# Reordering the first batch item of a Sinkhorn-sorted attention fused with a maxout feed-forward

## The chip, the cores and the metric

The kernel runs on one core of one Trainium2 chip. The metric is the device time of one execution, in microseconds. The time before is the median of 7 runs.

## What is computed

```
P = sort_net                              # 4 x 8 x 8 x 8, one 8x8 matrix for each item and head
for _ in range(5): P = exp(P - max); rows normalised; columns normalised
k_sorted, v_sorted = P applied over the 8 blocks of 96 tokens of k and v
scores = q_block . k_sorted_block^T / 8   # block by block, 96 x 96
x_attn = softmax(scores) . v_sorted       # 4 items x 768 tokens x (8 heads x 64)
h1 = x @ w1 ; h2 = x @ w2                 # 3072 tokens, 512 -> 1024
out = maximum(h1, h2) @ w_out             # 1024 -> 512
```

The kernel uses maximum(h1, h2) = relu(h1 - h2) + h2. It forms w1 - w2 once (`w_difference`, a quarter of the columns at a time), so that the first product needs one pass, and w2 @ w_out once (`w2_transposes`, `w_product`), so that h2 never appears.

## The kernel before

The four items (b) are processed one after the other, software-pipelined: while the feed-forward of item b runs, the attention of item b+1 is spread among its products. Item 0 has nothing to hide behind, so its order is written out by hand, statement by statement, at lines 682 to 713. All instructions of an engine run in the order in which they are written; `manual_schedule` keeps the written order, and the waits between engines are added by the framework.

The steps of one item, by the names used in the code and in the prediction:

- `sort_k(b, t)`, t = 0 to 2, and `sort_v(b, t)`, t = 0 to 3: block-diagonal products that mix the blocks of k and v, and an eviction on ACT or DVE into `kT` or `v_sb`. All value sorts must be evicted before the first values step.
- `q_transposes(b, half)`: for items 0 and 1 24 PE transposes (one more matmul ahead of them for item 0) and an eviction into `qT`; each half serves two of the four head pairs.
- `scores(b, u)` (SC, u = 0 to 7): 8 small matmuls and one exp on ACT. u = 4 * ih + hp, where hp is the head pair and ih the half of the blocks. hp 0 and 1 need the first half of q, hp 2 and 3 the second.
- `values(b, u)` (VA): 8 small matmuls, then a reciprocal and a multiplication on DVE, which give `x`.
- `x_transposes(b, t)` (TR): for item 0 8 PE transposes and an eviction into `xT`; for later items a DMA transpose on the SP queue. TR t needs values 2t and 2t+1. TR 0 and 1 serve token half 0, TR 2 and 3 token half 1.
- `moe_h(b, ch, t)`: the first product of token half ch, column tile t: 8 matmuls of 384 columns and a relu into `g`. `moe_h_products` issues a part of them: the parts (0, 2) need TR 0 only, the parts (1, 3) need TR 1. Tile t needs `w_difference(t)`. Differences 0 and 1 are on GpSimd (POOL), 2 and 3 on DVE.
- `w2_transposes(t, eng)`: 16 PE transposes and an eviction into `w2T`.

Every step that uses TensorE takes one of four PSUM tiles ("ps", two banks each); a step waits until the tile that it was given has been evicted. A number as the last argument of `scores`, `values` or `moe_h_products` puts that many columns of matmuls with zeros (`keep_streaming`) ahead of the step.

After the hand-written order come the selection copies and then the loop over items. In it `units` are the products of the feed-forward, and the planner adds `steps` of the next item in proportion to the units' costs. For item 0 units 0 and 1 are empty, units 2 to 7 are the remaining h tiles, units 8 to 11 the w products. `tail` names steps that follow a certain unit of item 0: the remaining work of item 0, the turning of v (`turn`), the block diagonals of the other items, the key sorts of item 1, and loads (`load_rest` is q of item 1 and k of item 2). Where an eviction has no engine given, `pick` chooses ACT or DVE from two running totals of planned time. All loads are issued by POOL, outputs by SP.

## Time and profile before

| what | value |
|---|---|
| median of 7 runs | 171.18 us (170.94 to 171.74) |
| profiled execution, its own time | 170.94 us |
| its span | 169.1 us |
| PE busy | 161.7 us (96% of the span) |
| ACT busy | 85.8 us (51%) |
| DVE busy | 75.8 us (45%) |
| POOL busy | 29.1 us (17%) |
| granted TensorE clock | 1.00 |
| DMA moved | 23.11 MB |

The profile is one execution, recorded by hardware. Times in its rows are in microseconds from the start of the span. PE is TensorE's matmuls and PEld its weight loads, DVE is VectorE, ACT is ScalarE, POOL is GpSimd, SP is SyncE. The rows of the timeline have start, length, engine, line, operation, output and inputs, shapes and count; in square brackets stands the engine's idle time before the row and what ended it. The ends of matmuls are modelled, so that neighbours seem to overlap; the distance from start to start says what a block costs.

### The profile page before, as it was taken

How to read it: one execution, taken by the hardware profiler on the slowest of the kernel's cores; microseconds unless marked ns; L12 is line 12 of the kernel's file. 1: busy time of each engine (PE TensorE's matmuls, PEld its weight loads, DVE VectorE, ACT ScalarE, POOL GpSimd, SP SyncE). 2: the span in 40 equal slices, each digit the busy share in tenths (PEclk: the TensorE clock that was granted, in tenths of full speed). 3: DMA queues.
4: the chain of work that ended last, by engine and by line, in shares of the span. 5: the costliest groups of instructions: out<-in, count | busy, mean ns of one | idle time of the engine just before them, and what ended most of it. 6: DMA issues, size and time to landing. Idle time of an engine off the chain costs nothing.

```text
span 169.1 us, 4528 instructions
## 1 busy us (share of the span) xinstructions
PE 161.7 (96%) x2001; PEld 97.2 (57%) x2019; DVE 75.8 (45%) x174; ACT 85.8 (51%) x104; POOL 29.1 (17%) x44
## 2 busy tenths in 40 slices
PE   7999989999999999999999999999999999999991
PEld 7948655567565554566664545557545455654451
DVE  5978765938363369437743443205442160000011
ACT  4587668686565352266775415456615416652020
POOL 7866584242312002100000000000000000000000
PEclk9999999999999999999999999999999999999999
DMA  3999999999999994899700253690054255000333
GB/s 51 204 203 198 200 207 207 218 204 206 217 214 205 205 206 94 174 156 237 159 0 4 63 155 131 95 292 17 0 35 139 47 176 171 0 0 0 124 141 111
DMA packets 30243, 23.11 MB, mean 137 GB/s; under 512 B 16720, under 2 KB 25168, under 8 KB 30224
## 3 DMA queue, kind: packets, MB, share of 16 engines
q0 software_dynamic: 10880, 12.59, 44.4%
q1 hardware_dynamic: 19200, 10.17, 24.7%
q8 instruction: 16, 0.26, 0.6%
q10 hardware_dynamic: 144, 0.07, 0.1%
q14 instruction: 3, 0.02, 0.0%
HBM read 25.17 MB, written 6.29 MB: 186 GB/s over the span
## 4 chain that ended last, share of the span: by engine, by line
PE 84%; DVE 9%; ACT 2%; issue 2%; DMA 1%
PE out_ps L617 35%; PE h_ps L590 23%; PE wc_ps L570 4%; PE o_ps L488 4%; PE k_ps L394 4%; PE s_ps L461 4%; PE v_ps L415 2%; PE fill_ps L82 2%; PE tq_ps L369 1%; ACT e L469 1%; PE v_ps L436 1%; DVE x L505 1%; PE tw_ps L551 1%; DVE qT L110 1%; DMA p_sb<-in_sort_net_dram 1%
## 5 line engine op out<-in xcount | busy, mean ns | idle before, releaser
L617 PE MATMUL out_ps<-wo_sb,g 128*128 128x512 bf16 (+2 forms) x188 | 47.0, 370 | 1.1 <-issue 0.3
L590 PE MATMUL h_ps<-xT,w_sb 128*128 128x384 bf16 x256 | 45.0, 326 | 0.4 <-ACT xT L108 0.3
L590 PEld LDWEIGHTS <-w_sb 128*128 128x128 bf16 x256 | 23.9, 98 | 16.1 <-issue 0.7
L108 ACT COPY o<-out_ps 128x1024 f32<-128x1024 f32 x11 | 11.1, 1012 | 40.4 <-issue 22.8
L604 ACT ACTIVATE g<-h_ps 128x768 bf16<-128x768 f32 x27 | 21.9, 811 | 15.0 <-PE h_ps L590 15.0
L469 ACT ACTIVATE e<-s_ps 96x768 bf16<-96x768 f32 x32 | 24.3, 804 | 7.7 <-PE s_ps L461 7.6
L617 PEld LDWEIGHTS <-g 128*128 128x128 bf16 x200 | 16.9, 98 | 15.7 <-DVE x L505 0.4
L617 PE MATMUL out_ps<-wc,xT 128*128 128x512 bf16 (+2 forms) x100 | 24.8, 370 | 0.1
L505 DVE TENSOR_TENSOR x<-o_ps,rs 96x512 bf16<-96x512 f32 x32 | 22.0, 687 | 1.1
L499 DVE RECIPROCAL rs<-o_ps 96x8 f32<-96x8 f32 x32 | 6.5, 202 | 32.2 <-PE o_ps L488 32.1
L617 PEld LDWEIGHTS <-xT 128*128 128x128 bf16 x100 | 9.6, 97 | 11.2
L488 PEld LDWEIGHTS <-e 96*128 96x128 bf16 x256 | 11.7, 98 | 7.0 <-ACT e L469 1.2
L488 PE MATMUL o_ps<-v_sb,e 96*128 96x65 bf16 x256 | 13.1, 193 | 0.4 <-ACT e L469 0.3
L652 DVE COPY o<-out_ps 128x512 f32<-128x512 f32 (+1 forms) x2 | 1.2, 624 | 25.0 <-PE out_ps L617 25.0
L110 DVE CAST v_sb<-v_ps 96x1024 bf16<-96x1024 f32 x8 | 9.6, 1215 | 4.2 <-PE v_ps L415 3.4
L110 DVE CAST kT<-k_ps 128x1024 bf16<-128x1024 f32 x5 | 6.0, 1222 | 11.3 <-PE k_ps L394 11.3
L461 PEld LDWEIGHTS <-kT 64*128 64x128 bf16 x256 | 6.3, 94 | 6.6 <-issue 5.9
L136 POOL DMA_DIRECT2D q_raw<-in_q_dram x7 | 6.4, 934 | 19.5 <-DVE rs L499 14.0
L108 ACT CAST v_sb<-v_ps 96x1024 bf16<-96x1024 f32 x8 | 8.0, 1006 | 3.2 <-PE v_ps L415 1.9
L461 PE MATMUL s_ps<-qT,kT 64*128 64x96 bf16 x256 | 9.0, 204 | 0.5 <-DVE qT L110 0.4
L82 PEld LDWEIGHTS <-fill 128*128 128x128 bf16 x99 | 8.2, 117 | 1.8 <-DVE fill L73 1.2
L82 PE MATMUL fill_ps<-fill 128*128 128x138 bf16 x88 | 7.5, 265 | 1.2 <-DVE fill L73 1.2
(77 smaller groups left out, 137.9 us busy)
## 6 DMA issues: line engine op xcount, KB each, us to landing
out_dram<-o SPq DMA_DIRECT2D x11, 512.0 KB, 3.0
k_raw<-in_k_dram POOLq DMA_DIRECT2D x12, 256.0 KB, 12.0
v_raw<-in_v_dram POOLq DMA_DIRECT2D x6, 384.0 KB, 11.7
q_raw<-in_q_dram POOLq DMA_DIRECT2D x3, 768.0 KB, 11.0
w_sb<-in_moe_w_dram POOLq DMA_DIRECT2D x4, 256.0 KB, 9.3
w_sb<-in_moe_w_dram POOLq DMA_DIRECT2D x2, 512.0 KB, 11.3
wo_sb<-in_moe_w_out_dram POOLq DMA_DIRECT2D x2, 512.0 KB, 14.8
v_raw<-in_v_dram POOLq DMA_DIRECT2D x3, 256.0 KB, 4.8
```

What stands on the lines that cost most here:

```text
L82: nc.tensor.matmul(ps[:, 0:w], w0, fill[:, 0:w], start=True, stop=True)
L108: nc.scalar.copy(out=out_ap, in_=in_ap)
L110: nc.vector.tensor_copy(out=out_ap, in_=in_ap)
L394: nc.tensor.matmul(ps[r0 : r0 + 64, m * 64 : (m + 1) * 64], kv[r0 : r0 + 64, t * 16 + m, :], bd_k[b][r0 : r0 + 64, :], start=True, stop=True,)
L461: nc.tensor.matmul(ps[:, h2 * 512 + ii * 128 : h2 * 512 + ii * 128 + BLK], kT[b][rows, (hp * 8 + i) * BLK : (hp * 8 + i) * BLK + 128], rhs ...
L469: nc.scalar.activation(out=e[:, 0 : 8 * BLK].rearrange("p (t c r) -> p t c r", t=8, r=R), in_=ps[0:BLK] .rearrange("p (t f) -> p t f", t=8 ...
L488: nc.tensor.matmul(ps[:, h2 * 512 + ii * 65 : h2 * 512 + (ii + 1) * 65], e[:, (h2 * 4 + ii) * BLK : (h2 * 4 + ii) * BLK + 128], v_sb[:, m0 ...
L505: nc.vector.tensor_tensor(out=x, in0=ov[:, :, :, 0:D], in1=rs.to_broadcast([BLK, 2, 4, D]), op=ALU.mult,)
L570: nc.tensor.matmul(ps[:, 0:512], w2T[:, fb, dmt * 128 : (dmt + 1) * 128], wo_sb[:, fb, :], start=(fb == 0), stop=(fb == NFB - 1),)
L590: nc.tensor.matmul(h_ps[t][:, m * 512 : m * 512 + TCH], w1_sb[:, hp, fb * 128 : (fb + 1) * 128], xT[:, b % 2, ch, hp % 2, hp // 2, :], sta ...
L604: nc.scalar.activation(out=g, in_=src, func=AF.Relu)
L617: nc.tensor.matmul(dst, g_tiles[b, ch, m // 2][:, m % 2, off : off + 128] if m < NFB else xT[:, b % 2, ch, hp % 2, hp // 2, off : off + 12 ...
```

## The change

In item 0, value sort 3 moves ahead of scores 0, scores 0 and 1 follow each other, and scores 4 moves ahead of values 0. The scores, values and x transposes of token half 1 move up among the h tiles: scores 5, 6 and 7 each one or more blocks earlier, values 6 and 7 and TR 2 into the hand-written order ahead of unit 2. The first half of h tile 1 is no longer issued apart: `moe_h(0, 0, 1)` is whole. The two w differences on DVE and the first w2 transposes come later. The zeros ahead of scores 0 (1024 columns) and values 0 (512) go, those ahead of values 2 grow from 512 to 1024, and values 3 gets 512. In `tail`, what followed unit 3 follows unit 2, and the key sorts of item 1 move from behind unit 7 to behind unit 8.

```diff
     sort_v(0, 2, 0, "A")
-    scores(0, 0, 1024)
     sort_v(0, 3, 0, "D")
+    SC[0]()
     SC[1]()
     q_transposes(0, 1, "D")
-    values(0, 0, 512)
+    SC[4]()
+    VA[0]()
     scores(0, 2, 1024)
     VA[1]()
     SC[3]()
-    values(0, 2, 512)
-    VA[3]()
+    values(0, 2, 1024)
     x_transposes(0, 0, "A")
-    SC[4]()
+    values(0, 3, 512)
+    SC[5]()
     moe_h_products(0, 0, 0, (0, 2), 512)
     x_transposes(0, 1, "A")
     VA[4]()
-    moe_h_products(0, 0, 1, (0, 2))
-    SC[5]()
+    SC[6]()
     moe_h(0, 0, 0, "A", (1, 3))
+    SC[7]()
+    VA[5]()
+    moe_h(0, 0, 1, "A")
+    x_transposes(0, 2, "A")
+    VA[6]()
     w_difference(2)
-    VA[5]()
-    moe_h(0, 0, 1, "A", (1, 3))
-    SC[6]()
+    VA[7]()
     w2_transposes(0, "D")()
     w_difference(3)
-    SC[7]()
...
     tail = {
-        2: [VA[6], TR[2], VA[7]],
-        3: [TR[3], lambda: w2_transposes(1, "A")(), load_rest],
+        2: [TR[3], lambda: w2_transposes(1, "A")(), load_rest],
...
-        7: [lambda t=t: sort_k(1, t) for t in range(3)] + [lambda: turn(second, 72)],
+        7: [lambda: turn(second, 72)],
+        8: [lambda t=t: sort_k(1, t) for t in range(3)],
```

## The prediction
> **What bounds the kernel now.** I read the page first (engine shares, then its chain), then the windows table, to find the stage that the edit can move, then the timeline of that stage.

> ```profile
> PE 161.7 (96%) x2001; PEld 97.2 (57%) x2019; DVE 75.8 (45%) x174; ACT 85.8 (51%) x104; POOL 29.1 (17%) x44
> PE 84%; DVE 9%; ACT 2%; issue 2%; DMA 1%
> ```

> TensorE is the bound, and it also carries 84% of the chain that ends last. The whole 9% of DVE on the chain lies before 34 us, apart from one spot at 63 to 67 us. So a reordering of the first item can only win by taking TensorE's waits out of that early stage. In the windows (columns after the stretch: its busy sum, then PE, PEld, DVE, ACT, POOL, clock, DMA):

> ```profile
> 16.00:18.00 2.00, 1.84 (x55) 1.44 (x50) 1.00 (x2) 1.48 (x3) 0.82 (x2) 1.00 1.45 200
> 20.00:22.00 2.00, 1.66 (x33) 1.18 (x33) 1.89 (x6) 1.44 (x2) 1.39 (x2) 1.00 1.29 207
> 22.00:24.00 2.00, 1.59 (x27) 1.09 (x28) 1.57 (x4) 1.15 (x3) 2.00 (x2) 1.00 1.25 211
> 32.00:34.00 2.00, 1.76 (x16) 0.98 (x16) 1.55 (x4) 1.14 (x2) 0.53 (x1) 1.00 1.05 216
> 36.00:38.00 2.00, 2.00 (x16) 1.06 (x14) 1.54 (x2) 1.27 (x2) 1.21 (x2) 1.00 1.12 207
> ```

> PE has holes up to 34 us and none at 36: from there on, whatever the first stage saves passes to the end. The timeline names the holes:

> ```profile
> 16.09 0.64 PE L415 MATMUL v_ps<-bd,v_dc 64*128 64x64 bf16 x16
> 17.21 0.35 PE L461 MATMUL s_ps<-qT,kT 64*128 64x96 bf16 x8 [0.16 <-DVE qT L110]
> 18.04 1.22 DVE L110 CAST v_sb<-v_ps 96x1024 bf16<-96x1024 f32 x1 [0.89 <-PE v_ps L415]
> ...
> 20.18 0.35 PE L461 MATMUL s_ps<-qT,kT 64*128 64x96 bf16 x8 [0.25 <-DVE qT L110]
> ...
> 22.12 0.42 PE L488 MATMUL o_ps<-v_sb,e 96*128 96x65 bf16 x8 [0.28 <-ACT e L469]
> ...
> 23.77 0.81 PE L590 MATMUL h_ps<-xT,w_sb 128*128 128x384 bf16 x4 [0.29 <-ACT xT L108]
> ...
> 33.67 0.52 PE L526 MATMUL tx_ps<-ident,x 96*128 96x96 bf16 x8 [0.24 <-DVE x L505]
> ...
> 34.92 1.30 PE L590 MATMUL h_ps<-xT,w_sb 128*128 128x384 bf16 x7
> ```

> To see: 16.09 is value sort 2, the last step that both orders share; 34.92 is the first h product of token half 1 (call it h10; h02 is half 0, tile 2), which both orders reach with the same work behind them. Between them lie 18.83 us. Value sort 3's eviction starts only at 18.04, after DVE has sat idle 0.89; the second q eviction, and with it scores 2 (20.18), queues behind it.

> **The sum for that stretch.** Durations from the rows, PE start to start where work is dense: a value sort 0.515 (two from 14.10 to 15.13), a q half 0.95, scores 0.28, values 0.245, x transposes 0.345, an h tile 1.30 (a half 0.65), a w2 group 0.89 to 1.0, 512 filler columns 0.213. Two sorts 1.03, one q half 0.95, eight scores 2.24, eight values 1.96, four x groups 1.38, four h tiles 5.2 and two w2 groups 1.85 make 14.6. Fillers are 3584 columns, 1.49. So 2.7 us are waits (some under the fillers, so the profile's holes are smaller).

> **The change, step by step.** I lay the new order out with those durations and these: from a block's PE start to its eviction's start 0.67 (value sort), 1.07 (q), 0.38 (scores), 0.45 (values), 0.53 (x), 0.86 (h half), 1.51 (h tile), 1.10 (w2); evictions ACT exp 0.80, xT 0.80, relu 0.81, v 1.01; DVE v 1.22, q 0.95, reciprocal plus multiply 0.92, w_difference 0.69, w2T 1.22; 0.05 from an engine's end to PE; 0.06 overlap of neighbours on ACT and DVE. A PSUM tile takes the buffer that comes free first (4 exist). The same rules laid over the old order give 35.20 for h10, against 34.92 in the trace, and from 23.77 to 34.92 they take 11.26 for 11.15: good to 0.3 us. New order (PE start; the wait before it; what that is):

> ```
> v3  16.61             DVE evicts 17.28-18.50 (was 18.04-19.26)
> SC0 17.20  0.08 qT    SC1 17.48
> q1  17.82  0.06 buffer of v2;   DVE 18.89-19.84 (was 19.18-20.12)
> SC4 18.77  VA0 19.05 (was 19.31)   x0 19.78-20.70
> SC2 19.89  0.17 q1 eviction, fill 1024 under it (was 20.18)
> VA1 20.17  SC3 20.42  VA2 21.18 0.05 buffer, after fill 1024
> TR0 21.61  0.19 x1 (was 22.38)   VA3 22.17  SC5 22.41
> h00 first half 22.99  0.08 xT0 (was 23.77)
> TR1 23.64  VA4 23.99  SC6 24.23
> h00 second half 25.02  0.51 xT1 (ACT 24.17-24.97)
> SC7 25.67  VA5 25.95  h01 26.20  TR2 27.50  VA6 27.84  VA7 28.09
> w2 group 0  28.57  0.23 buffer of h01, relu ends 28.52
> h02 29.89  0.38 w_difference(2), DVE 29.15-29.84
> TR3 31.19  w2 group 1 31.54  h03 32.54 0.05 w_difference(3), ends 32.49
> h10 33.84  (was 34.92)
> ```

> Removed: the waits of values 3 on its exp (0.50 by the rules), of h00 on xT0 (0.54), of TR3 on x7 (0.54: x7 now has two other blocks and h02 ahead of its reader), of h03 on the buffer of h02 (0.23), of values 5 on exp 5 (0.30), and 512 filler columns net (0.21). Added: h00's second half waits 0.51, since h01's first half no longer stands between TR1 and it; behind it on PE queue SC7, VA5 and h01. h02 waits 0.38, since w_difference(2) moved behind x6 on DVE; before, it ran at 26.77 in DVE's idle time and cost nothing. The 0.23 of w2 group 0 is new. Waits fall by about 0.9, fillers by 0.21: h10 comes 1.08 earlier. Against the rules' own 35.20 it would be 1.36. Adding the same durations without the overlaps on DVE gave me 34.15, a gain of 0.77. I take 1.0.

> **What costs nothing, and under which cover.** The selection and mask copies (0.8 us of DVE, about 32.4 to 33.2) finish ahead of the first h10 relu on DVE. The planner's engine choices: I added up its two running totals in both orders, and no eviction changes its engine. Key sorts of item 1 behind the first w product: the same 1.64 us of PE, now at about 41.0 instead of 40.54; their third k_raw piece was issued at about 25.8 and landed 13.1 later (the DMA view, issue to landing), at 38.9. Without that cover (sorts left in unit 7, third piece needed at about 40.5) 1.6 us of margin would still stand. The last v turn goes ahead of the key evictions on DVE: 0.82 us earlier for the value sorts, no one waits for it. Queues: first-item steps issue no DMA (its transposes are on PE), so SP's queue is not passed. load_rest (one q, three k transfers) is emitted one h tile earlier, but POOL's issues wait for landings: q_raw at 27.21 and k_raw at 29.48, 32.30, 34.58 each follow the landing of the transfer eight issues before (w_sb 26.6, wo_sb 29.2 and 32.0, v_raw 34.3). PE has long been done with these buffers, so POOL keeps its times. q_raw(1) lands at 27.21 + 15.9 = 43.1 and is read at about 46.2. At 63 to 67 us DVE is late by its own queue, not by a landing: q_raw(2) lands at 51.59 + 10.6 = 62.2 against a read at 65.16. So the gain is not eaten there.

> [...]

> ```profile
> 4.50:5.50 1.00, 1.00 (x11) 1.00 (x10) 1.00 1.09 217
> 5.50:6.50 1.00, 1.00 (x20) 1.00 (x18) 1.00 1.03 205
> ```

> These are windows of the filler line alone at the start: 11 per us, then 20: PE reached its full rate near 5.5 us. [...] The old order runs without filler from 12.46 to 16.66; the new one from 12.46 to 19.30, 6.8 us of small matmuls and some 50 transposes. [...] I take the row: no cost, and 1.5 for the range.

> **Other unknown.** The buffer each PSUM tile gets. Second-best choices, one at a time, cost nothing (most) up to 0.73 (the q half waiting for value sort 3's eviction at 18.50); no choice makes PE start earlier than the first free one. I take the first-free rule, which reproduces the old order's waits, and keep 0.7 for the range.

> **Rivals.** [...] (2) A wait in place of the old one: worse buffers for q1 or h01 (+0.7 or +0.55) or DVE's w_differences later by their 0.69; the gain shrinks to 0.2 to 0.4, 170.9. For it: DVE is at 1.89 of 2 us in 20:22. (3) The gain is given back after 34 us by a landing or by the key sorts among the w products: 171.2. Against it: the margins above.

> **How the numbers follow.** Profiled run 170.94 (span 169.1 plus 1.8 around it), 0.24 under the median of 171.18. From the median: 171.18 - 1.0 = 170.2. Chances: main 0.68 (169.7 to 170.7); rival 2 0.13 (a third of it faster by over 0.2%); rival 3 0.06; rival 1 0.13. 0.2% is 0.34 us, about what a measurement of this kernel can tell from no change. Faster 0.68 + 0.04 = 0.72, same 0.09 + 0.06 = 0.15, slower 0.13. Range: down to a gain of 1.5, up to no change and a little more: 169.6 to 171.3.

> **What would show it.** After: value sort 3's eviction near 17.3; second scores group with q1 near 19.9; first h product near 23.0; a wait of about 0.5 on xT before h00's second half; waits on w_difference ahead of h02; h10 near 33.8 to 34.2; clock 1.00 at 16 to 24; the same distance from h10 to the end. Wrong if matmul rates halve near 19 us, if h10 is later than 34.6, or if k sorts wait.

## The result, and the profile after

The changed kernel takes 170.63 us in the median of 24 runs (170.02 to 171.38), against 171.36 us for the kernel before in 61 runs on the same chips (170.94 to 172.22). The ratio is 0.9957, with a 95% interval of 0.9947 to 0.9968: 0.73 us less, between 0.55 and 0.91. Forecast were 1.0 us less and 170.2 us, in a range of 169.6 to 171.3. Medians in this document are of all runs; the ratios leave out runs more than 1.5% above the fastest of their kernel (one of e4, one of e7, two of e8).

The profiled execution of the changed kernel is the slowest of its runs (171.38 us, span 169.5), that of the kernel before one of the fastest (170.94, span 169.1). So the two spans must not be set against each other; they have to be taken apart by stage first. The page, engine shares and chain:

```profile
PE 162.1 (96%) x2000; PEld 98.3 (58%) x2018; DVE 75.9 (45%) x174; ACT 85.7 (51%) x104; POOL 28.6 (17%) x44
PE 92%; DVE 3%; issue 2%; ACT 1%
```

DVE's share of the chain fell from 9% to 3%. The windows of the changed kernel (the columns are as before):

```profile
16.00:18.00 2.00, 1.98 (x61) 1.75 (x62) 1.77 (x3) 1.48 (x2) 1.40 (x2) 1.00 1.45 195
20.00:22.00 2.00, 1.79 (x33) 1.01 (x30) 1.81 (x5) 1.53 (x3) 1.57 (x1) 1.00 1.30 205
22.00:24.00 2.00, 2.00 (x37) 1.52 (x36) 1.78 (x5) 1.62 (x3) 1.94 (x1) 1.00 1.24 206
24.00:26.00 2.00, 1.63 (x30) 1.24 (x28) 1.05 (x3) 1.50 (x3) 2.00 (x5) 1.00 1.24 207
30.00:32.00 2.00, 1.75 (x19) 1.15 (x17) 1.97 (x5) 0.21 (x1) 0.41 (x1) 1.00 1.19 229
32.00:34.00 2.00, 2.00 (x31) 1.68 (x29) 2.00 (x8) 1.61 (x3) 0.53 (x1) 1.00 1.02 210
36.00:38.00 2.00, 2.00 (x16) 1.06 (x14) 1.70 (x2) 0.81 (x2) 0.87 (x2) 1.00 1.10 201
```

The holes at 22 and 32 us are closed. New ones stand at 24 and 30 us, where the prediction had placed the two added waits. Its timeline names them:

```profile
16.81 1.10 PE L415 MATMUL v_ps<-bd,v_dc 64*128 64x64 bf16 x32
...
17.95 1.22 DVE L110 CAST v_sb<-v_ps 96x1024 bf16<-96x1024 f32 x1
...
20.61 0.51 PE L461 MATMUL s_ps<-qT,kT 64*128 64x96 bf16 x8 [0.21 <-DVE qT L110]
...
23.89 0.81 PE L590 MATMUL h_ps<-xT,w_sb 128*128 128x384 bf16 x4
...
25.94 0.81 PE L590 MATMUL h_ps<-xT,w_sb 128*128 128x384 bf16 x4 [0.37 <-ACT xT L108]
...
30.88 1.48 PE L590 MATMUL h_ps<-xT,w_sb 128*128 128x384 bf16 x8 [0.25 <-DVE w_sb L194]
...
33.45 2.77 PE L590 MATMUL h_ps<-xT,w_sb 128*128 128x384 bf16 x16
...
37.46 0.20 PE L303 MATMUL pe<-p_bf,sel_v 32*128 32x64 bf16 x1
```

The last of these rows in the kernel before:

```profile
37.62 0.20 PE L303 MATMUL pe<-p_bf,sel_v 32*128 32x64 bf16 x1
```

All times here are 0.72 us late against the kernel before, whatever the order: in this execution value sort 2, the last shared step, starts at 16.81 instead of 16.09. Counted from value sort 2, the eviction of value sort 3 starts at 1.14 (before 1.95), scores 2 at 3.80 (4.09), the second half of h tile 0 waits on xT, and h tile 2 waits on w_difference. h10, the first h product of token half 1, starts 17.95 us behind value sort 2, instead of 18.83. (In a merged row its start isn't shown; it is taken as the block-diagonal row, L303, less the two h tiles between. They take 2.70, the distance from 34.92 to 37.62 before, so h10 starts at 34.76 here.) So in the stage that the change touches, this pair of profiles shows a gain of 0.88 us. The spans then add up: +0.72 from the start, -0.88 in the stage, +0.60 from one gap at 81.7 us, together +0.44. By the time of the span h10 at 34.76 is later than 34.6, which the prediction named as a sign of being wrong; less the 0.72 it is at 34.04, inside the 33.8 to 34.2 that it expected.

The gap and its neighbours, changed kernel:

```profile
81.25 0.61 PE L436 MATMUL v_ps<-bd,v_dc 64*128 64x64 bf16 x30
...
82.28 0.21 PE L436 MATMUL v_ps<-bd,v_dc 64*128 64x64 bf16 x2 [0.42 <-issue]
...
82.42 1.47 PE L590 MATMUL h_ps<-xT,w_sb 128*128 128x384 bf16 x8
```

The same value sort and h tile before, 0.57 us apart instead of 1.17:

```profile
81.40 0.64 PE L436 MATMUL v_ps<-bd,v_dc 64*128 64x64 bf16 x32
...
81.97 1.48 PE L590 MATMUL h_ps<-xT,w_sb 128*128 128x384 bf16 x8
```

PE stops inside one step, between two equal matmuls that need nothing new; the profile puts it down to "issue". The second such gap is hidden in the row at 20.61: it lasts 0.51 us where the same eight matmuls took 0.35 before, since 0.16 us lie between the starts of the first and the second of them. What these are was the main question of the experiments.

### The profile page after: what moved, and what is told of

It reads as the page before. It is cut to its first block, busy times and chain, and to the rows that moved or that the text cites. A ratio compares the mean times of both kernels' runs of the same rounds, so it can differ in the third digit from the quotient of the medians.

```text
span 169.5 us, 4526 instructions
## 1 busy us (share of the span) xinstructions
PE 162.1 (96%) x2000; PEld 98.3 (58%) x2018; DVE 75.9 (45%) x174; ACT 85.7 (51%) x104; POOL 28.6 (17%) x44
## 4 chain that ended last, share of the span: by engine, by line
PE 92%; DVE 3%; issue 2%; ACT 1%
PE out_ps L617 35%; PE h_ps L590 25%; PE fill_ps L82 6%; PE o_ps L488 4%; PE wc_ps L570 4%; PE k_ps L394 4%; PE s_ps L461 4%; PE v_ps L415 2%; PE tq_ps L369 2%; PE v_ps L436 1%; PE tx_ps L526 1%; ACT v_sb L108 1%; DVE qT L110 1%; PE k_ps L82 1%; DVE q_pair L343 1%
## 5 line engine op out<-in xcount | busy, mean ns | idle before, releaser
L590 PE MATMUL h_ps<-xT,w_sb 128*128 128x384 bf16 x256 | 44.7, 326 | 0.6 <-ACT xT L108 0.4
L590 PEld LDWEIGHTS <-w_sb 128*128 128x128 bf16 x256 | 24.0, 98 | 16.4 <-DVE w_sb L194 0.4
L108 ACT COPY o<-out_ps 128x1024 f32<-128x1024 f32 x11 | 11.1, 1012 | 40.4 <-issue 22.8
L469 ACT ACTIVATE e<-s_ps 96x768 bf16<-96x768 f32 x32 | 24.3, 804 | 6.2 <-PE s_ps L461 6.2
L617 PEld LDWEIGHTS <-g 128*128 128x128 bf16 x200 | 16.9, 98 | 15.7 <-DVE x L505 0.4
L505 DVE TENSOR_TENSOR x<-o_ps,rs 96x512 bf16<-96x512 f32 x32 | 22.0, 687 | 1.1
L499 DVE RECIPROCAL rs<-o_ps 96x8 f32<-96x8 f32 x32 | 6.5, 203 | 33.8 <-PE o_ps L488 33.6
L488 PEld LDWEIGHTS <-e 96*128 96x128 bf16 x256 | 11.6, 98 | 6.0 <-ACT e L469 0.2
L488 PE MATMUL o_ps<-v_sb,e 96*128 96x65 bf16 x256 | 12.9, 193 | 0.0
L110 DVE CAST kT<-k_ps 128x1024 bf16<-128x1024 f32 x5 | 6.0, 1223 | 12.3 <-PE k_ps L394 12.3
L110 DVE CAST v_sb<-v_ps 96x1024 bf16<-96x1024 f32 x8 | 9.7, 1216 | 3.0 <-PE v_ps L415 1.7
L82 PEld LDWEIGHTS <-fill 128*128 128x128 bf16 x98 | 8.8, 125 | 1.6 <-DVE fill L73 1.2
L108 ACT CAST v_sb<-v_ps 96x1024 bf16<-96x1024 f32 x8 | 8.0, 1006 | 3.2 <-PE v_ps L415 1.9
L461 PEld LDWEIGHTS <-kT 64*128 64x128 bf16 x256 | 6.1, 94 | 6.2 <-issue 5.2
L82 PE MATMUL fill_ps<-fill 128*128 128x138 bf16 x88 | 8.3, 281 | 1.2 <-DVE fill L73 1.2
L461 PE MATMUL s_ps<-qT,kT 64*128 64x96 bf16 x256 | 8.9, 204 | 0.3 <-DVE qT L110 0.2
```

Source lines behind the costliest of these rows:

```text
L82: nc.tensor.matmul(ps[:, 0:w], w0, fill[:, 0:w], start=True, stop=True)
L108: nc.scalar.copy(out=out_ap, in_=in_ap)
L110: nc.vector.tensor_copy(out=out_ap, in_=in_ap)
L461: nc.tensor.matmul(ps[:, h2 * 512 + ii * 128 : h2 * 512 + ii * 128 + BLK], kT[b][rows, (hp * 8 + i) * BLK : (hp * 8 + i) * BLK + 128], rhs ...
L469: nc.scalar.activation(out=e[:, 0 : 8 * BLK].rearrange("p (t c r) -> p t c r", t=8, r=R), in_=ps[0:BLK] .rearrange("p (t f) -> p t f", t=8 ...
L488: nc.tensor.matmul(ps[:, h2 * 512 + ii * 65 : h2 * 512 + (ii + 1) * 65], e[:, (h2 * 4 + ii) * BLK : (h2 * 4 + ii) * BLK + 128], v_sb[:, m0 ...
```

## The experiments

Each run was set against the kernel before on the same chip. Beside the ratio I give the distance from value sort 2 to h10 in the run's profile, which is free of the start and of everything behind h10. The last column is what the prediction's rules give for it.

| kernel | ratio to before (95%) | h10 behind value sort 2 | by the rules |
|---|---|---|---|
| before | 1 | 18.83 | 19.11 |
| changed | 0.9957 (0.9947 to 0.9968) | 17.95 | 17.75 |
| e1 w_difference(2) early | 0.9926 (0.9901 to 0.9952) | 17.33 | 17.32 |
| e2 key sorts in unit 7 | 0.9945 (0.9923 to 0.9967) | 18.23 | 17.75 |
| e3 head only | 0.9989 (0.9968 to 1.001) | 18.54 | 18.65 |
| e4 no fillers | 0.9955 (0.9928 to 0.9981) | 18.92 | 17.75 |
| e5 tail only | 0.9959 (0.9943 to 0.9974) | 18.29 | 18.42 |
| e6 e1 and TR 2 later | 0.9923 (0.9898 to 0.9948) | 17.10 | 17.09 |
| e7 64 instructions fewer | 1.0255 (1.0225 to 1.0285) | 18.94 | 17.75 |
| e8 e6, shorter start | 1.0039 (1.0015 to 1.0062) | 18.05 | 17.09 |

**e1: is the new wait on w_difference real, and is it the last one?**

```diff
     VA[5]()
+    w_difference(2)
     moe_h(0, 0, 1, "A")
     x_transposes(0, 2, "A")
     VA[6]()
-    w_difference(2)
```

> The changed kernel with one move: w_difference(2) from behind values 6 to right behind values 5. Theory A (the lay-out with trace durations: the wait of h tile 2 on w_difference(2), 0.25 to 0.4 us, sits on PE's path): the difference runs on DVE at about 27.3 to 28.0 while PE does h tile 1, h tile 2 starts with no wait, and its successor h tile 3 is not held by the other difference; h10 (first h product of token half 1) starts 17.32 us behind value sort 2 where the changed kernel's lay-out has 17.75, so about 0.4 us faster than the changed kernel, ratio to before about 0.993. Rival B (the wait is replaced at once by the next one, the w2T eviction or a PSUM buffer): no gain over the changed kernel, ratio 0.9957 as that.

Measured: 169.92 us (10 runs), ratio 0.9926. Timeline of this kernel:

```profile
27.46 0.68 DVE L194 TENSOR_TENSOR w_sb<-w_sb 128x1024 bf16<-128x1024 bf16 x1
...
29.67 1.46 PE L590 MATMUL h_ps<-xT,w_sb 128*128 128x384 bf16 x8
```

The difference runs while DVE is free, h tile 2 has no wait in its row, and the distance is 17.33, as laid out. Theory A holds, rival B falls: the wait that the change had added cost all that it showed. The row and the distance decide this; in time the intervals of e1 and of the changed kernel still overlap a little. A stop as in the changed kernel came in this profile too, at 80.41, and took 0.94 us.

**e2: does the move of the key sorts matter?**

```diff
-        7: [lambda: turn(second, 72)],
-        8: [lambda t=t: sort_k(1, t) for t in range(3)],
+        7: [lambda t=t: sort_k(1, t) for t in range(3)] + [lambda: turn(second, 72)],
```

> The changed kernel with the key sorts of item 1 put back behind unit 7 (with the last v turn behind them, as before). Theory A (that move costs and gains nothing, since k_raw's third piece lands at about 39 us and PE does the same work in another order): ratio to before 0.9957 as the changed kernel, scores 1.0 starts at the same distance from value sort 2. Rival B (the move was needed: with PE about 0.2 to 0.9 us earlier the sorts would wait for a landing or for block diagonals): a PE wait ahead of the key sorts of 0.3 us or more, ratio 0.998 or above.

Measured: 170.31 us (12 runs), ratio 0.9945; its interval overlaps that of the changed kernel. No wait ahead of the key sorts (40.67, straight behind the h tiles). The first scores of item 1 start 36.37 us behind value sort 2 against 36.09, but this profile has a longer stop inside scores 2, which is in the same place as the changed kernel's. PE timeline of e2:

```profile
20.62 0.20 PE L461 MATMUL s_ps<-qT,kT 64*128 64x96 bf16 x1
21.06 0.34 PE L461 MATMUL s_ps<-qT,kT 64*128 64x96 bf16 x7 [0.25 <-issue]
```

One matmul, and the other seven only 0.44 us after its start. Less their stops (0.45 and 0.16) the two distances are 35.92 and 35.93. So the move of the key sorts costs and gains nothing; theory A holds. The order of work up to h10 is the same in both kernels, and yet h10 stands at 18.23 here and at 17.95 there: the stop accounts for that.

**e3 and e5: the two halves of the change.**

```diff
e3, against the kernel before:
-    scores(0, 0, 1024)
     sort_v(0, 3, 0, "D")
+    SC[0]()
     SC[1]()
     q_transposes(0, 1, "D")
-    values(0, 0, 512)
+    SC[4]()
+    VA[0]()
...
     x_transposes(0, 0, "A")
-    SC[4]()
```

> The kernel before with only the head of the change: value sort 3 ahead of scores 0 (without its 1024 filler columns), scores 4 ahead of values 0 (without its 512); all behind that in the old order. Theory A (lay-out): value sort 3's eviction and the second q eviction come 0.3 us earlier, values 0 to 3 and TR 0 follow, and h10 comes 0.46 us earlier: 18.65 against 19.11 from value sort 2 in the lay-out, ratio about 0.9975. Rival B (the head alone is absorbed: the h tiles' waits on w_difference and on exps take it back): h10 within 0.1 us of before, ratio 1.000. Rival C (clock): the filler-free stretch lowers the matmul rate near 19 us, slower than before.

```diff
e5, against the changed kernel:
-    sort_v(0, 3, 0, "D")
-    SC[0]()
+    scores(0, 0, 1024)
+    sort_v(0, 3, 0, "D")
     SC[1]()
     q_transposes(0, 1, "D")
-    SC[4]()
-    VA[0]()
+    values(0, 0, 512)
...
     values(0, 3, 512)
+    SC[4]()
```

> The changed kernel with the head of the old order: scores 0 with its 1024 filler columns ahead of value sort 3, values 0 with its 512 directly behind the second q half, scores 4 only behind values 3; all behind that as changed. Theory A (lay-out): TR 0 and with it the first h product come earlier by its place ahead of values 3, h10 starts 18.42 behind value sort 2 against 19.11 in the old order's lay-out and 17.75 in the changed one's, so about 60% of the gain, ratio about 0.997. Rival B (the head is what counts, the reordering of the h tiles only adds its own waits on xT and w_difference): h10 no earlier than before, ratio 1.000.

Measured: the head alone takes 0.29 us off the stage, the tail alone 0.54. In time the head alone is 170.97 (12 runs; the interval of its ratio includes 1), the tail alone 170.59 (8 runs). So most of the gain comes from the new order of the h tiles, scores and values; the head is worth some 0.3 us. Both rivals of "one half does it all" fall, by the stage of one profile each; the time of e3 alone could not tell. The clock stayed at full rate in e3's profile (mean 1.00), though its first filler comes behind values 0, as in the changed kernel.

**e4: are the fillers needed?**

```diff
-    scores(0, 2, 1024)
+    SC[2]()
-    values(0, 2, 1024)
+    VA[2]()
-    values(0, 3, 512)
+    VA[3]()
-    moe_h_products(0, 0, 0, (0, 2), 512)
+    moe_h_products(0, 0, 0, (0, 2))
```

> The changed kernel without the four fillers ahead of scores 2, values 2, values 3 and the first h product (3072 filler columns, which compute nothing). Theory A (fillers lie under waits, and the clock holds without them): no difference to the changed kernel, h10 at the same 17.75 of the lay-out (17.95 in the trace) behind value sort 2, or up to 0.2 us earlier, since the trace shows values 2 about 0.2 us late behind its filler; ratio 0.9945 to 0.996. Rival B (the clock gate needs them): half-rate matmuls for some 3.4 us near 19 to 26 us, ratio 1.000 or above.

Measured: 170.65 us (12 runs, 169.93 to 172.72). Windows of this kernel; the third number from the right is the granted clock:

```profile
22.00:24.00 2.00, 1.64 (x27) 1.19 (x28) 1.60 (x4) 1.60 (x3) 2.00 (x2) 0.81 1.23 205
24.00:26.00 2.00, 2.00 (x26) 1.56 (x25) 0.12 (x1) 0.56 (x1) 2.00 (x5) 0.50 1.24 208
```

The trace's clock record has half rate from 23.24 to 26.66, 3.41 us. The profile's h10 is 1.17 us behind the rules. Six of the 12 runs show a mean clock of 0.99 or less, and these are the ones above 171 us or at it; the six with 0.999 or 1.00 lie at 169.93 to 170.29. The changed kernel's runs never fall under 0.997. So without the fillers the clock decides from run to run, which is B. Where the clock held, A came near: the median of those six is 170.05, against 170.31 for e2, which has the same order up to h10, with the fillers, and ran on the same chip. Whether these 0.26 us are a cost of the fillers, or of the stop inside scores 2 that e2's profile has, isn't separated.

**e6: can the stage be made dense?** The kernel of e1, and TR 2 behind the first w2 group:

```diff
     moe_h(0, 0, 1, "A")
-    x_transposes(0, 2, "A")
     VA[6]()
     VA[7]()
     w2_transposes(0, "D")()
+    x_transposes(0, 2, "A")
     w_difference(3)
```

> The kernel of the early w_difference with one more move: TR 2 from behind h tile 1 to behind the first w2 group, so that values 6 and 7 reach DVE earlier and the w2 group takes an older PSUM buffer. Theory A (lay-out): no PE wait is left between h tile 1 and h10; h10 starts 17.09 behind value sort 2 against 17.32 (and 17.75 of the changed kernel), ratio to before about 0.9915. Rival B (PE already runs into limits that the lay-out does not hold, the loading of instruction blocks above all): no gain over the early w_difference, ratio 0.9926 or above, with PE gaps inside a block of equal matmuls.

Measured: 169.89 us (6 runs), ratio 0.9923; e1 on its chip had 0.9926, so the two can't be told apart in time, though the best run went from 169.59 to 169.37. Theory A holds in the stage, not in time. In the profile the stage has 17.10, by the rules 17.09. Windows of e6:

```profile
28.00:30.00 2.00, 2.00 (x42) 1.80 (x39) 1.91 (x6) 1.09 (x2) 0.63 (x2) 1.00 1.25 208
30.00:32.00 2.00, 2.00 (x30) 1.68 (x29) 2.00 (x5) 1.50 (x3) 0.33 (x1) 1.00 1.17 225
```

No hole is left behind h tile 1. This kernel has the shortest stage of all, and is about 1.3 us faster than the one before; its interval just touches that of the changed kernel.

**e7: what are the stops inside a step?** The stops end 2.2 to 2.6 us after the start of a transfer on the queue that the page calls "q8 instruction": 16 packets, 0.26 MB, so 16 KB each. If the stops are waits for these, they must move when the instruction stream is shifted.

```diff
-    keep_streaming(ps_f32("fill_ps"), 88 * 138, most=138)
+    keep_streaming(ps_f32("fill_ps"), 56 * 217, most=217)
```

> The changed kernel with the zeros at the very start cut in 56 matmuls of 217 columns in place of 88 of 138 (12152 columns for 12144): 64 PE instructions fewer, all else the same. Theory A (the gap inside scores 2, between its first and second matmul, and the gap inside a value sort at about 81.7 us are waits for the next 16 KB block of instructions): both places come 64 instructions later in the stream, so no gap between the first matmuls of scores 2, but one (if any) inside values 2 or TR 0, where PE waits for DVE anyway. h10 at 17.75 behind value sort 2. Rival B (the gap in scores 2 belongs to the wait on the q eviction or to memory): it stays between the same two matmuls.

Measured: 175.92 us (4 runs, 175.39 to 178.70), 2.55% slower than the kernel before, for work that is that of the changed kernel but for 64 PE instructions fewer. Timeline of e7:

```profile
15.79 0.75 PE L369 MATMUL tq_ps<-ident,q_raw 128*64 128x128 bf16 x20
...
19.72 0.30 PE L369 MATMUL tq_ps<-ident,q_raw 128*64 128x128 bf16 x4 [3.19 <-issue]
```

PE stops for 3.40 us inside the transposes of the first q half, whose inputs have long been there. The DMA view of e7 from 17.3 to 18.4 us has the one transfer on that queue between 11 us and the end of the stop (transfers, MB, share of the 16 engines):

```profile
q8 instruction: 1, 0.02, 5.5%
```

It starts at 17.35, and PE goes on 2.37 us later. The load starts are those of the queue's packet records in the trace. In the profiles that show such stops they behave alike (instruction number counted over PE's rows, matmuls and weight loads):

| kernel | stop (us) | length | PE row | load starts; PE goes on after |
|---|---|---|---|---|
| changed | 20.61 | 0.16 | 705 | 18.47; 2.30 |
| changed | 81.67 | 0.61 | 2488 | 79.91; 2.37 |
| e1 | 80.41 | 0.94 | 2497 | 78.91; 2.44 |
| e2 | 20.62 | 0.45 | 707 | 18.86; 2.20 |
| e7 | 16.32 | 3.40 | 449 | 17.35; 2.37 |
| e8 | 14.99 | 0.87 | 449 | 13.52; 2.34 |
| e8 | 21.10 | 0.96 | 704 | 19.70; 2.36 |
| e8 | 47.32 | 1.59 | 1469 | 46.34; 2.57 |

The rows are 256 apart, or a multiple of it, within nine rows (some records are missing), in all five kernels of the table: in them the boundaries stay in place and the work shifts over them. I had expected the next stop inside values 2; that was wrong, for I looked only at the boundary at row 705, and the one at 449 came to lie under work that can't wait. Rival B, a wait on the q eviction, falls: in e7 scores 2 starts at 24.90 behind the same wait for the q eviction, and its eight matmuls take 0.35 us with no gap among them. In e7 the clock went to half rate after the stop, from 20.32 to 23.73, which the stage pays a second time. Why the load started only at 17.35, about 6 us later than the first load of most other profiles (10.5 to 11.9), is settled in part by PE's rows. From row 193 to row 1473, the load for a boundary starts in all ten profiles only 0.6 to 4.5 us after PE has passed the boundary before it (further on the missing records blur the count). The zeros cut at the start stood ahead of row 193, so PE reaches that row at 13.29 in e7, in the midst of the key sorts, instead of 9.84 to 10.83 in eight of the others (12.40 in e8), and then needs only 3.03 us to row 449. The rest, a lag of 4.06 us where the other nine have 0.6 to 1.1 at this row, stays open; the DMA engines moved about 200 GB/s then, but they did so in the other kernels too.

**e8: the start.**

```diff
 e6 and
-    keep_streaming(ps_f32("fill_ps"), 88 * 138, most=138)
+    keep_streaming(ps_f32("fill_ps"), 78 * 138, most=138)
```

> The kernel of e6_wdiff_tr2 with 78 instead of 88 matmuls of zeros at the start. Theory A (where the clock goes to full rate late, at about 7 us, the zeros end at 9.5 us, after DVE is done, and hold PE back by up to 0.7 us; where early, DVE's chain is later than the zeros anyway): value sort 2 starts at 16.1 to 16.3 in all runs, the runs lie closer together, and the median falls by 0.1 to 0.4 us against e6_wdiff_tr2. Rival B (fewer zeros leave PE idle ahead of the third round and the clock falls back or rises later): slower, with matmul rates halved before 16 us or value sort 2 later than 16.9.

Measured: 172.02 us (12 runs), slower than before, ratio 1.0039. The first load again comes late, at 13.52, value sort 2 starts at 16.95, and this profile has three stops of the kind above, of 0.87 to 1.59 us, one of them at the transposes of item 1. Behind that one the clock record has half rate from 49.09 to 52.50. The profiled run took 174.21 us at a mean clock of 0.989; nine of the 12 runs have a clock of 0.996 or more and still take 171.51 to 172.37, so the fall of the clock is not what the median shows. PE timeline of e8:

```profile
47.32 0.24 PE L369 MATMUL tq_ps<-ident,q_raw 128*64 128x128 bf16 x1
48.91 1.30 PE L369 MATMUL tq_ps<-ident,q_raw 128*64 128x128 bf16 x23 [1.35 <-issue]
```

Theory A on the start can't be judged from it: 20 instructions fewer moved the block boundaries as well. Whether a shorter start with the boundaries in their old places would help stays open.

## Why the prediction was right

**The bound and the place.** PE's waits ahead of 34 us were what a new order could win, and what was won there passed to the end: from h10 to the value sort at 81.4 us there are 46.48 us before and 46.49 after the change, and behind the gap the two kernels keep step to 0.02 us. Right.

**The lay-out.** Its two added waits came at their places: 0.51 forecast for h tile 0's second half behind xT (0.37 in the row; 0.43 from the start of scores 6 at 25.23 less its 0.28), 0.38 for h tile 2 behind w_difference(2) (0.25 in the row; about 0.4 from the start of the w2 group at 29.57 less its 0.9). In four kernels without a visible stop or a fall of the clock in the stage (e1, e3, e5, e6) it came out within 0.13 us of the rules, twice within 0.01. That fits the assumption that each PSUM tile gets the first free buffer; the traces leave the buffer numbers out, so it was not seen directly.

**The term that was mis-sized.** The sum gave 1.08 for the stage; the profile shows 0.88, and the median 0.73. (The 1.08 sets the rules' new order against the trace's old one. The rules had made the old order 0.28 too long; that they would not do so with the new one was not known, and by the rules alone the gain would have been 1.36. In e3 and e5, each with one half of the old order, they are 0.11 and 0.13 too long, so the error belongs to the old halves; taking 1.0 and not 1.36 was in part luck.) Of the 0.20 in the stage 0.16 is the stop inside scores 2, read as a wait for a block of instructions (PE goes on 2.30 us after the load at 18.47), which the prediction did not have at all. A second stop took 0.60 in the profiled run behind h10. The start differs by 0.72 between these two profiles, whose work is the same up to value sort 2. How often such stops or a late start fall in the runs without a profile can't be seen, so the cause of the 0.15 between 0.88 and the median stays open.

**The clock.** I had taken it that the clock does not fall in the stretch without filler. The row behind that was the kernel before: no filler from 12.46 to 16.66, and a clock of 1.00 from 5.51 to 169.35. In the changed kernel it held: 1.00 in the profile from 7.13 to the end of the work, and 0.997 or more in every run. But e4 shows that this hangs on the fillers that remain: without the four of them, half of the runs lose clock, in the profiled one in this stage. The 1.5 us that the range holds for a fall of the clock, and rival 1 with its chance of 0.13, rest on a term that no run shows; what the runs show in its place is the fall in e4, half rate from 23.24 to 26.66, with h10 1.17 us behind the rules. Nor was the row the same case: before the change PE is busy all of 12.33 to 15.74, while the changed order has waits between its small matmuls (PE busy for 3.04 of the 3.41 us from 24.20 to 27.61).

**What was costed at nothing.** Planner choices, key sorts (e2), POOL's queue and q_raw's landing: right (q_raw of item 1 landed at 43.47 and was read at 47.08). One reading was off and did no harm: the third k_raw piece landed at 39.23 before the change, not 38.9, because the 13.1 is the median of two transfers. The rival "given back after 34 us" did occur in the profiled run, by a mechanism that it did not name.

## What to carry to other kernels

In a stage that waits on several engines, an order can be judged by hand from one profile: start-to-start lengths, the lag to each eviction, in-order queues and buffers taken as first-free gave the stage lengths of e1, e3, e5 and e6 to 0.13 us. When steps move on the critical engine, a helper instruction that was hidden beside them, here w_difference(2) on DVE, can come to be waited for: move it too, to where its engine is idle. In e1 that gave another 0.4 us (0.6 with the stop that this profile did not have). And when filler instructions are cut, the work behind them can come to lie under other stops, as in e7 (64 PE instructions fewer, a stop of 3.40 us) and e8 (20 fewer than e6, three stops of 0.87 to 1.59 us): compare such variants by profile, not by time alone.

## What was not expected of the hardware

**The start.** The first clock record at full rate begins at 5.51 us in the profile before and at 7.13 in that of the changed kernel; the windows of the filler line of the latter show it:

```profile
5.50:6.50 1.00, 1.00 (x12) 1.00 (x10) 1.00 1.01 201
6.50:7.50 1.00, 1.00 (x14) 1.00 (x12) 1.00 1.00 193
7.50:8.50 1.00, 1.00 (x20) 1.00 (x18) 1.00 1.14 213
```

Twenty matmuls per us come only in the third window, where the kernel before had them from 5.5 on. The zeros end at 9.47 instead of 8.69, and value sort 2 starts at 16.81 instead of 16.09. In e1, e5 and e6 the record begins at 4.4 to 4.7 and value sort 2 starts at 16.1 to 16.2; in e2 at 7.16, and 16.82. So among these six profiles value sort 2 starts up to 0.7 us later where the clock rises later, as much as the change itself is worth.

**The clock's steps.** Every fall of the clock in these ten profiles comes a whole number of steps of 3.41 us after the first record at full rate: 5 steps in e4 (6.18 to 23.24), 4 in e7 (6.66 to 20.32), 13 in e8 (4.71 to 49.09), and likewise at the end of each run (48 steps, 163.84 us, in the profile before and in that of the changed kernel). The step just ahead of a fall was thin: PE is busy for 2.48 us of it in e4 (19.83 to 23.24), 0.60 in e7 (16.90 to 20.32) and 2.07 in e8 (45.67 to 49.09), while the thinnest step in the changed kernel's stage has 3.04 (24.20 to 27.61). Busy time alone does not tell a fall: the changed kernel's step from 164.14 to 167.56, output products and then nothing, has 2.02, and no fall follows. The first rise lies between 4.4 and 7.2 us in these profiles; if the steps count from it in every run, the same thin stretch is cut at other places from run to run. That would explain why only half of e4's runs lose clock, but the runs without a profile don't show it.
